# Pooled attention into a Mish FFN: the row maximum in two chains, its transposes in row tiles, and part of the row sums on TensorE

## Chip, cores and metric

The kernel runs on one core of one Trainium2 chip. The metric is device time in microseconds (us) of one execution, without host work.

## What is computed

```python
def _attn_ref(q, k, v):                     # q, k, v: (4, 8, 1152, 64) float32
    q_pool = q.reshape(B, H, S // 2, 2, D).mean(axis=3)
    scores = (1.0 / np.sqrt(D)) * np.matmul(q_pool, k.transpose(0, 1, 3, 2))
    scores = scores - np.max(scores, axis=-1, keepdims=True)
    attn = np.exp(scores)
    attn = attn / (np.sum(attn, axis=-1, keepdims=True) + 1e-09)
    return np.matmul(attn, v)

def _moe_ref(x, w_in, w_out):               # x: (2304, 512), d_ff = 2048
    h = x @ w_in
    sp = np.where(h > 20.0, h, np.log1p(np.exp(np.minimum(h, 20.0))))
    return (h * np.tanh(sp)) @ w_out
```

Neighbouring queries are averaged in pairs, so each of the 32 (batch, head) pairs has 576 queries and 1152 keys. The attention output, its heads side by side, is the input of the FFN.

## The kernel before

**Attention.** There are 32 steps. A step `i` takes two heads (`j` = 0, 1, on the partition halves 0 to 63 and 64 to 127 of the inputs) and half of their queries (288 columns, `HQ`). Scores are made transposed: keys on partitions, queries along the free axis. The 1152 keys are nine chunks `c` of 128. For each chunk TensorE computes `s` (`QK`, 128 x 2 x 288, two PSUM banks), with the two heads in the two 64-row halves of the array; ScalarE copies it into `T3` in SBUF (`CP`); VectorE folds it into a running maximum `rmax` (`MX`). Two PSUM tiles (`psS`) hold scores, so a chunk's scores need the copy and the maximum of an earlier chunk done.

The maximum over keys runs across partitions. So `MT` transposes the 576 columns of `rmax` on TensorE in five blocks of 128, `TMAX` reduces them on VectorE to a column `m`, and `MB`/`MBb` transpose `m`, broadcast along the free axis, back into a PSUM tile `Mb` that holds each query's maximum on all 128 partitions. `SUB` subtracts it (VectorE, in four groups of 2, 2, 2 and 3 chunks), `EXP` exponentiates on ScalarE, `PV` multiplies by the values on TensorE (two column halves, again one for each head). GpSimd (POOL) adds the nine chunks of exponentials together (`ADD` 0 to 4, the last two of half width), `FIN0` sums that over the partitions with a matmul by ones, and `FLN`, `FEX`, `FE`, `FU`, `FX` divide and write into `xT`.

**FFN.** After step 31 come 18 blocks of 256 tokens by 16 slices of d_ff, in float32r with hi and lo parts: `H_` (12 matmuls), `A_g`/`A_gh` (Mish on ScalarE), `D_gl`, `O_` (6 matmuls). Some of the weight conversion (`conv`) and of the splitting of `xT` (`split_h`, `split_l`) lies between attention steps.

**What sets the order.** The order on every engine is written out by hand: `STEP` gives for each function of a step its time, in units of one step, for even and odd `i`; `FILL` overrides it for the first steps, `END` for the last. All entries are sorted by time and issued in that order; each engine then works its own queue from front to back and waits only for semaphores. An instruction that waits on TensorE therefore holds up all matmuls behind it. A warm-up (`first`) keeps TensorE busy until the first inputs are there.

The fold that the change rewrites is a single chain:

```python
def MX(i, c):
    if c == 1:
        rmaxs[i, 1] = p2.tile([P, 2, HQ], F32, tag="rmax", name=f"rmax{i}")
    r = rmaxs[i, 1]
    dve.tensor_tensor(r, ss[i, c], T3[:, i % 2, 0] if c == 1 else r, ALU.max)
```

Of the kernel before, what the change touches and what calls it, by code (L numbers as in the profile page):

```python
# [22 lines left out]
def tile_pooled_attention_then_mish_ffn(ctx: ExitStack, tc: tile.TileContext, q, k, v, moe_w_in, moe_w_out, out):  # L23
# [42 lines left out]
    if True:  # L66
# [60 lines left out]
        WARM2 = ((64, 64), (64, 64), (64, P), (64, 64), (P, 64), (64, 64))  # L127

        def first():
            qk_tiles(0)  # L130
            if NWARM:
# [3 lines left out]
                x = ps1.tile([P, 2, 512], F32, tag="Mb", name="warm2")  # L135
                for k, m in WARM2:
                    for r in range(0, P, k):
                        for c in range(0, P, m):
                            pe.matmul(x[c:c + m, r // 64, 0:P], ident[r:r + k, 0:m], ident[r:r + k], start=True, stop=True)
# [776 lines left out]
```

## Time and profile before

| | |
|---|---|
| three runs | 854.29, 854.6 and 857.56 us, median 854.6 |
| the profiled execution | 854.77 us, of which the span from first to last instruction is 852.7 us |
| attention, until the last step's maximum | 0 to 428 us |
| change-over and FFN | 428 to 852.7 us |
| busy over the span | PE 97%, PEld 67%, DVE 70%, ACT 60%, POOL 53% |
| the same from 150 to 200 us | PE 98%, DVE 98%, POOL 96%, ACT 88% |

PE is the matmuls of TensorE and PEld its weight loads, DVE is VectorE, ACT is ScalarE, POOL is GpSimd. In the attention stage nearly every engine is busy nearly all the time, in the FFN stage only PE is. Matmuls are pipelined, so the distance from the start of one group to the start of the next says more than a busy share: a group of matmuls that waits counts as busy.

### The profile page before, as it was taken

Reading aid. Unit: us, or ns where it says so; the run is one execution under the profiler, and the core shown is the slowest. Engines: PE = TensorE matmul, PEld = TensorE weight load, DVE = VectorE, ACT = ScalarE, POOL = GpSimd, SP = SyncE. Lnnn points to the kernel's source line nnn. Section 1 sums busy time; section 2 is a strip of 40 time slices with the busy share of each in tenths; the row PEclk is TensorE's granted clock in tenths of the full one; section 3 lists DMA queues with packets and bytes.
Section 4 is the critical chain, followed back from the end, with each engine's and each line's share of the span. In section 5 each row is a group of like instructions: output and inputs, shape, how many; then the busy total and the mean of one; then the engine's idle time right before and its main releaser. Section 6 shows DMA issues by size and latency. Waiting matters only on the chain. (4 is left out here: it accounts for less than half of the span.)

```text
span 852.7 us, 13965 instructions
## 1 busy us (share of the span) xinstructions
PE 826.5 (97%) x5422; PEld 572.9 (67%) x5422; DVE 592.7 (70%) x810; ACT 513.0 (60%) x916; POOL 449.8 (53%) x268
## 2 busy tenths in 40 slices
PE   7899999999999999999989999999999999999997
PEld 4344444444444444444468899999999999989896
DVE  6999999999999999999978634444553444422222
ACT  5788898888888888988865643333333333222221
POOL 0799999999999999999876401110111101100000
PEclk9899999999999999999999999999999999999999
DMA  5320122211222202222001111110211111001102
GB/s 213 109 83 15 71 84 84 84 41 44 85 84 85 74 13 83 84 84 78 1 1 50 59 41 50 50 50 25 75 50 50 50 48 34 20 26 50 45 30 74
DMA packets 16913, 50.70 MB, mean 59 GB/s; under 512 B 1616, under 2 KB 6480, under 8 KB 16848
## 3 DMA queue, kind: packets, MB, share of 16 engines
q1 hardware_dynamic: 16848, 49.81, 16.9%
q8 instruction: 43, 0.70, 0.3%
q14 instruction: 22, 0.18, 0.1%
HBM read 45.09 MB, written 4.72 MB: 58 GB/s over the span
## 5 line engine op out<-in xcount | busy, mean ns | idle before, releaser
L742 DVE TENSOR_TENSOR gl<-g,gh 128x256 fp32r<-128x256 f32 x144 | 67.3, 467 | 226.1 <-ACT gh L737 199.9
L154 PE MATMUL s<-qT,kT 64*128 64x288 f32 x1152 | 200.1, 449 | 7.3 <-DVE rmax L171 3.2
L164 ACT COPY T<-s 128x576 f32<-128x576 f32 x288 | 180.2, 635 | 40.5 <-DVE rmax L171 24.0
L732 ACT ACTIVATE g<-h 128x256 f32<-128x256 f32 x144 | 55.7, 387 | 244.7 <-PE h L727 244.7
L204 DVE TENSOR_TENSOR T<-T,Mb 128x1152 f32<-128x1152 f32 (+1 forms) x128 | 191.2, 1495 | 0.9 <-PE Mb L198 0.9
L208 ACT ACTIVATE T<-T 128x1152 f32<-128x1152 f32 (+1 forms) x128 | 164.4, 1286 | 25.4 <-DVE T L204 25.2
L226 PE MATMUL pv<-T,vn 128*64 128x288 f32 x1152 | 174.5, 420 | 3.5 <-ACT pvs L237 3.5
L171 DVE TENSOR_TENSOR rmax<-s,rmax 128x576 f32<-128x576 f32 x224 | 168.6, 753 | 11.1 <-ACT T L164 1.8
L405 POOL TENSOR_TENSOR wl<-wt,wh 128x512 fp32r<-128x512 f32 x32 | 41.9, 1308 | 247.1 <-ACT wh L402 203.2
L216 POOL TENSOR_TENSOR acc<-acc,T 128x1152 f32<-128x1152 f32 x64 | 169.0, 2640 | 6.0 <-ACT T L208 3.1
L727 PE MATMUL h<-xh,wh 128*128 128x256 f32 x576 | 162.1, 281 | 0.0
L727 PE MATMUL h<-xh,wl 128*128 128x256 f32 x576 | 161.8, 281 | 0.0
L727 PE MATMUL h<-xl,wh 128*128 128x256 f32 x576 | 161.6, 281 | 0.0
L154 PEld LDWEIGHTS s<-qT,kT 64*128 64x128 f32 x1152 | 91.8, 189 | 99.7 <-ACT T L164 49.4
L226 PEld LDWEIGHTS pv<-T,vn 128*64 128x64 f32 x1152 | 71.7, 137 | 80.4 <-issue 42.2
L727 PEld LDWEIGHTS h<-xh,wh 128*128 128x128 f32 x576 | 108.7, 189 | 8.0 <-issue 1.3
L727 PEld LDWEIGHTS h<-xl,wh 128*128 128x128 f32 x576 | 108.8, 189 | 6.0
L727 PEld LDWEIGHTS h<-xh,wl 128*128 128x128 f32 x576 | 109.2, 189 | 0.0
L214 POOL TENSOR_TENSOR acc<-T 128x1152 f32<-128x1152 f32 x32 | 84.7, 2648 | 21.1 <-ACT gh L737 6.0
L760 PE MATMUL o<-wh,gh 128*128 128x512 f32 x146 | 57.8, 396 | 1.0 <-ACT xT L772 1.0
L760 PE MATMUL o<-wl,gh 128*128 128x512 f32 x146 | 57.6, 394 | 0.0
L760 PE MATMUL o<-wh,gl 128*128 128x512 f32 x146 | 57.3, 392 | 0.0
(373 smaller groups left out, 987.1 us busy)
## 6 DMA issues: line engine op xcount, KB each, us to landing
vn<-in_v_dram SPq DMA_DIRECT2D x16, 576.0 KB, 6.3
kT<-in_k_dram SPq DMA_DIRECT2D x15, 576.0 KB, 5.0
qn<-in_q_dram SPq DMA_DIRECT2D x15, 576.0 KB, 3.8
ri<-in_moe_w_in_dram SPq DMA_DIRECT2D x16, 512.0 KB, 3.5
ro<-in_moe_w_out_dram SPq DMA_DIRECT2D x16, 512.0 KB, 3.5
out_dram<-xT SPq DMA_DIRECT2D x18, 256.0 KB, 2.6
qh<-in_q_dram SPq DMA_DIRECT2D x2, 288.0 KB, 5.0
kT<-in_k_dram SPq DMA_DIRECT2D x1, 256.0 KB, 4.7
```

The source lines that it names most:

```text
L154: pe.matmul(s[:, j, 0:HQ], kT[64 * j:64 * j + 64, c], qT[64 * j:64 * j + 64, hf], start=True, stop=True,)
L164: act.copy(T3[:, i % 2, c], ss[i, c])
L171: dve.tensor_tensor(r, ss[i, c], T3[:, i % 2, 0] if c == 1 else r, ALU.max)
L204: dve.tensor_tensor(x, x, Mbs[i][:, :, 0:HQ].unsqueeze(1).to_broadcast([P, w, 2, HQ]), ALU.subtract)
L208: act.activation(x, x, AF.Exp, scale=0.0625)
L214: pool.tensor_tensor(accs[i], t[:, 0:2], t[:, 2:4], ALU.add)
L216: pool.tensor_tensor(accs[i], accs[i], t[:, 2 * n + 2:2 * n + 4], ALU.add)
L226: pe.matmul(pvs[i][64 * j:64 * j + 64, 0:HQ], vn[:, j, c, :], T3[:, i % 2, c, j], start=(pvn[i] == 1), stop=(pvn[i] == NC),)
L727: pe.matmul(h[:, 0:UT], a, b, start=(m == 0), stop=(m == len(seq) - 1))
L732: act.activation(g, hs[bu, f], AF.Mish)
L742: dve.tensor_tensor(gl, ch.pop((bu, f)), f32(gs[bu, f][0]), ALU.subtract)
L760: pe.matmul(os_[bu][t], x, y, start=(first and m == 0), stop=(last and m == 2))
```

## The change

1. **Two chains.** Chunks 1, 3, 5, 8 are folded into `rmax0` (seeded with the copied chunk 0), chunks 4 and 6 into `rmax1` (seeded with the copied chunk 2). `MX` of chunk 7 takes `rmax1` and writes its result over the scores of chunk 7 in PSUM; `MXF` folds that into `rmax0`. A step still has eight maxima.
2. **Transposes in row tiles.** `MT` becomes ten transposes of 64 partitions x 128 columns, two for each block, in the two 64-row halves of the array. It takes every fourth column of `rmax` for blocks 0 to 3. `MB` (with `MBb` merged into it) becomes nine such transposes that write every fourth column of `Mb`; `Mb` is now 576 columns in a row. `TMAX` and `SUB` read the new layouts.
3. **Sums.** POOL makes only `ADD` 0, 1, 2. The two halves of the accumulator and chunk 8 of `T3` are summed over partitions by three matmul pairs (`FIN0`, `FIP1`, `FIP0`) that accumulate in one PSUM tile, where there was one pair.
4. **Order.** `STEP` is written anew, with the same times for even and odd steps nearly everywhere and the score chunks mostly in pairs; `FILL`, the pooling of `q` (`QP`), the loads of `q`, the splits (`XE`, `XL`) and the release of PSUM (`REUSE`) have new times. The warm-up is 19 transposes where it was 6 transposes and 20 small matmul instructions.

```diff
-    NWARM = 6
+    NWARM = 19
...
-        WARM2 = ((64, 64), (64, 64), (64, P), (64, 64), (P, 64), (64, 64))
...
+        CHAIN, SEED, FOLD = ((1, 3, 5, 8), (4, 6, 7)), (0, 2), 7
+        PIECES = 2
...
         def MX(i, c):
-            if c == 1:
-                rmaxs[i, 1] = p2.tile([P, 2, HQ], F32, tag="rmax", name=f"rmax{i}")
-            r = rmaxs[i, 1]
-            dve.tensor_tensor(r, ss[i, c], T3[:, i % 2, 0] if c == 1 else r, ALU.max)
-
-        MBLK = (0, 128, 224, 352, 448)
+            n = [c in a for a in CHAIN].index(True)
+            first = c == CHAIN[n][0]
+            if first:
+                rmaxs[i, n] = p2.tile([P, 2, HQ], F32, tag=f"rmax{n}", name=f"rmax{i}_{n}")
+            r = rmaxs[i, n]
+            x = r
+            if first:
+                x = T3[:, i % 2, SEED[n]]
+            dve.tensor_tensor(ss[i, c] if c == FOLD else r, ss[i, c], x, ALU.max)
+
+        def MXF(i):
+            r = rmaxs[i, 0]
+            dve.tensor_tensor(r, ss[i, FOLD], r, ALU.max)
...
         def MT(i):
-            rm = rmaxs.pop((i, 1)).rearrange("p a b -> p (a b)")
-            t = ps1.tile([P, 1024], F32, tag="Mb", name=f"mt{i}")
-            for n, a in enumerate(MBLK):
-                pe.transpose(t[:, n * P:(n + 1) * P], rm[:, a:a + P], ident)
+            rm = rmaxs.pop((i, 0)).rearrange("p a b -> p (a b)")
+            t = ps1.tile([P, 2, 512], F32, tag="Mb", name=f"mt{i}")
+            for n in range(5):
+                for r in range(2):
+                    h = slice(64 * r, 64 * r + 64)
+                    x = rm[h, n:4 * P:4] if n < 4 else rm[h, W - P:W]
+                    pe.transpose(t[:, r, 64 * n:64 * n + 64], x, ident[h, h])
...
         def MB(i):
             m = Ts.pop(i)
-            Mb = ps1.tile([P, 2, 512], F32, tag="Mb", name=f"Mb{i}")
-            Mbs[i] = Mb, m
-            for n, j, a in ((0, 0, 0), (1, 0, 128), (3, 1, 64), (4, 1, 160)):
-                pe.transpose(Mb[:, j, a:a + P], m[:, n:n + 1].to_broadcast([P, P]), ident)
-
-        def MBb(i):
-            Mb, m = Mbs[i]
-            for k, j, a in ((0, 0, 224), (64, 1, 0)):
-                pe.transpose(Mb[:, j, a:a + 64], m[k:k + 64, 2:3].to_broadcast([64, P]), ident[k:k + 64, k:k + 64])
-            Mbs[i] = Mb
+            Mb = ps1.tile([P, 1024], F32, tag="Mb", name=f"Mb{i}")
+            for n in range(5):
+                for r in range(n // 4, 2):
+                    h = slice(64 * r, 64 * r + 64)
+                    a = 256 + 256 * r + n
+                    x = Mb[:, a:256 + a - n:4] if n < 4 else Mb[:, 768:832]
+                    pe.transpose(x, m[h, n:n + 1].to_broadcast([64, P]), ident[h, h])
+            Mbs[i] = Mb[:, 256:832]
...
-                pool.tensor_tensor(accs[i][:, 0], accs[i][:, 0], t[:, 8] if n == 3 else accs[i][:, 1], ALU.add)
+                pool.tensor_tensor(accs[i][:, 0], accs[i][:, 0], t[:, 8] if n + PIECES == 3 else accs[i][:, 1], ALU.add)
...
+        def SUM(i, a, n):
...
+            for j in range(2):
+                pe.matmul(fin[i][64 * j:64 * j + 64, 0:HQ], ones, a[:, j], start=(n == 0), stop=(n == PIECES))
+
+        def FIP0(i):
+            SUM(i, T3[:, i % 2, 8], 0)
+
+        def FIP1(i):
+            SUM(i, accs[i][:, 1], 1)
+
         def FIN0(i):
...
+            SUM(i, accs.pop(i)[:, 0], PIECES)
...
-            (MX, 7, 0.2982, 0.2113),
+            (MX, 7, 0.3034, 0.3034),
...
-        LW, REUSE = -0.5, -0.544
+        LW, REUSE = -0.5, -0.678
```

What that makes of the order shows best on the two engines that are fullest. The rows below are one step in the middle of the attention stage. On VectorE (`L204` and `L208` are `SUB`, `L263` and `L275` `FE`, `L282` `FX`, `L185` and `L191` `TMAX`), before, from the maximum's reduction on:

```order
L185 TENSOR_REDUCE m_1648<-mt_1637 128x5
L171 TENSOR_TENSOR rmax_1643<-s_2_1645,rmax_1643 128x576
L282 SCALAR_TENSOR_TENSOR xT<-Sb_1602,pvs_1590 128x288
L204 TENSOR_TENSOR T_98<-T_98,Mb_1654 128x1152
L171 TENSOR_TENSOR rmax_1643<-s_3_1664,rmax_1643 128x576
L204 TENSOR_TENSOR T_98<-T_98,Mb_1654 128x1152
L171 TENSOR_TENSOR rmax_1643<-s_4_1678,rmax_1643 128x576
L171 TENSOR_TENSOR rmax_1643<-s_5_1682,rmax_1643 128x576
L204 TENSOR_TENSOR T_98<-T_98,Mb_1654 128x1152
L171 TENSOR_TENSOR rmax_1643<-s_6_1698,rmax_1643 128x576
L171 TENSOR_TENSOR rmax_1643<-s_7_1705,rmax_1643 128x576
L171 TENSOR_TENSOR rmax_1643<-s_8_1724,rmax_1643 128x576
```

and on the same engine after:

```order
L191 TENSOR_REDUCE m_1799<-mt_1783 128x5
L170 TENSOR_TENSOR rmax_0_1781<-s_3_1796,rmax_0_1781 128x576
L170 TENSOR_TENSOR rmax_1_1818<-s_4_1802,T_98 128x576
L208 TENSOR_TENSOR T_98<-T_98,Mb_1806 128x1152
L170 TENSOR_TENSOR rmax_0_1781<-s_5_1830,rmax_0_1781 128x576
L170 TENSOR_TENSOR rmax_1_1818<-s_6_1833,rmax_1_1818 128x576
L208 TENSOR_TENSOR T_98<-T_98,Mb_1806 128x1152 x2
L170 TENSOR_TENSOR rmax_0_1781<-s_8_1859,rmax_0_1781 128x576
L170 TENSOR_TENSOR s_7_1854<-s_7_1854,rmax_1_1818 128x2x288
L174 TENSOR_TENSOR rmax_0_1781<-s_7_1854,rmax_0_1781 128x576
```

Of two maxima in a row the second used to read what the first had just written; now that is so only in the last pair of a step, chunk 7 and `MXF`. On TensorE (`L154` and `L149` are the scores, `L226` and `L230` `PV`, `L180` and `L185` `MT`, `L193`, `L198` and `L202` `MB`, `L248` and `L252` the sums; `x2` are the two matmuls of one chunk), before:

```order
L180 MATMUL mt_1637<-identr,rmax_1538 128x128 x5
L154 MATMUL s_2_1645<-qT_1450,kT_1451 128x288 x2
L193 MATMUL Mb_1654<-identr,m_1648 128x128 x4
L198 MATMUL Mb_1654<-identr,m_1648 128x64 x2
L154 MATMUL s_3_1664<-qT_1450,kT_1451 128x288 x2
L226 MATMUL pv_1598<-T_98,vn_1495 64x288 x4
L154 MATMUL s_4_1678<-qT_1450,kT_1451 128x288 x2
L154 MATMUL s_5_1682<-qT_1450,kT_1451 128x288 x2
L226 MATMUL pv_1598<-T_98,vn_1495 64x288 x6
```

and after:

```order
L149 MATMUL s_2_1900<-qT_1578,kT_1579 128x288 x2
L185 MATMUL mt_1907<-identr,rmax_0_1781 128x64 x10
L149 MATMUL s_3_1920<-qT_1578,kT_1579 128x288 x2
L149 MATMUL s_4_1926<-qT_1578,kT_1579 128x288 x2
L202 MATMUL Mb_1930<-identr,m_1923 128x64 x9
L230 MATMUL pv_1868<-T_98,vn_1620 64x288 x4
L149 MATMUL s_5_1950<-qT_1578,kT_1579 128x288 x2
L149 MATMUL s_6_1954<-qT_1578,kT_1579 128x288 x2
L230 MATMUL pv_1868<-T_98,vn_1620 64x288 x4
L252 MATMUL Sb_1965<-T_98,cst 64x288 x2
L252 MATMUL Sb_1965<-acc_1871,cst 64x288 x2
```

Scores, `MT` and `MB` now stand together in one stretch of 64-row instructions, where before each of them stood between others of another shape; two more pairs of sums stand beside the `PV`. At the start of the program, TensorE ran before (`L134` and `L139` are the warm-up):

```order
L134 MATMUL warm<-identr 128x128 x6
L139 MATMUL warm_114<-identr 64x128 x8
L139 MATMUL warm_114<-identr 128x128 x2
L139 MATMUL warm_114<-identr 64x128 x10
L154 MATMUL s_0_143<-qT_105,kT_106 128x288 x2
```

and it runs now:

```order
L132 MATMUL warm<-identr 128x128 x19
L149 MATMUL s_0_135<-qT_105,kT_106 128x288 x2
L149 MATMUL s_1_138<-qT_105,kT_106 128x288 x2
L149 MATMUL s_2_144<-qT_105,kT_106 128x288 x2
L149 MATMUL s_3_151<-qT_105,kT_106 128x288 x2
```

The warm-up is 19 transposes in a row, and the first scores follow them directly.

## Rows read from the trace of the kernel before

**Rows 1.** Busy time by stretch, all engines: us, busy us (instructions), clock, DMA.
```profile
20.00:40.00 20.00, 17.23 (x93) 7.76 (x95) 18.20 (x23) 14.42 (x20) 14.90 (x9) 0.83 0.35 115
...
150.00:200.00 50.00, 48.98 (x336) 24.17 (x332) 48.95 (x58) 43.92 (x64) 48.05 (x28) 1.00 0.21 72
...
420.00:440.00 20.00, 15.36 (x117) 9.62 (x114) 16.34 (x16) 14.18 (x22) 15.10 (x10) 1.00 0.00 1
...
550.00:600.00 50.00, 50.00 (x323) 45.25 (x321) 22.33 (x43) 16.63 (x45) 6.37 (x5) 1.00 0.16 53
```
**Rows 2.** The line of `TMAX`, steps 3 to 31: count, durations, first and last start.
```profile
L185 DVE TENSOR_REDUCE m<-mt x29: 812/815/826, 61.6 to 428.1; 128x5 f32<-128x640 f32 x29
```
**Rows 3.** VectorE in order of time within one step: start, length, line, instruction, count.
```profile
216.03 1.94 DVE L204 TENSOR_TENSOR T<-T,Mb 128x1728 f32<-128x1728 f32 x1
217.89 0.46 DVE L263 SCALAR_TENSOR_TENSOR Sb<-Sb,rs 128x288 f32<-128x288 f32 x1
218.26 0.74 DVE L171 TENSOR_TENSOR rmax<-s,T 128x576 f32<-128x576 f32 x1
218.92 0.81 DVE L185 TENSOR_REDUCE m<-mt 128x5 f32<-128x640 f32 x1
219.65 0.74 DVE L171 TENSOR_TENSOR rmax<-s,rmax 128x576 f32<-128x576 f32 x1
220.32 0.45 DVE L282 SCALAR_TENSOR_TENSOR xT<-Sb,pvs 128x288 f32<-128x288 f32 x1
220.69 1.35 DVE L204 TENSOR_TENSOR T<-T,Mb 128x1152 f32<-128x1152 f32 x1
221.96 0.75 DVE L171 TENSOR_TENSOR rmax<-s,rmax 128x576 f32<-128x576 f32 x1
...
223.88 1.61 DVE L171 TENSOR_TENSOR rmax<-s,rmax 128x576 f32<-128x576 f32 x2
225.41 1.34 DVE L204 TENSOR_TENSOR T<-T,Mb 128x1152 f32<-128x1152 f32 x1
```
**Rows 4.** TensorE in order of time, three places of the attention stage.
```profile
204.45 0.71 PE L226 MATMUL pv<-T,vn 128*64 128x288 f32 x4
205.09 0.77 PE L180 MATMUL mt<-identr,rmax 128*128 128x128 f32 x5
205.78 1.24 PE L154 MATMUL s<-qT,kT 64*128 64x288 f32 x8
206.96 0.65 PE L193 MATMUL Mb<-identr,m 128*128 128x128 f32 x4
207.54 0.27 PE L198 MATMUL Mb<-identr,m 64*128 64x64 f32 x2
207.74 0.71 PE L226 MATMUL pv<-T,vn 128*64 128x288 f32 x4
...
209.67 2.16 PE L226 MATMUL pv<-T,vn 128*64 128x288 f32 x16
211.76 1.24 PE L154 MATMUL s<-qT,kT 64*128 64x288 f32 x8
...
220.37 0.27 PE L198 MATMUL Mb<-identr,m 64*128 64x64 f32 x2
220.48 0.70 PE L154 MATMUL s<-qT,kT 64*128 64x288 f32 x4
```
**Rows 5.** One of GpSimd's half-width adds, grouped by line, 60 to 400 us.
```profile
L218 POOL TENSOR_TENSOR acc<-acc 128x576 f32<-128x576 f32 x26 | 36.8, 1417 | 2.0
```
**Rows 6.** The start, in order of time: warm-up, first scores, a stall of VectorE.
```profile
1.62 1.00 PE L134 MATMUL warm<-identr 128*128 128x128 f32 x6 [1.62 <-DVE cst L72]
...
6.24 3.61 PE L154 MATMUL s<-qT,kT 64*128 64x288 f32 x16
...
31.21 0.76 DVE L171 TENSOR_TENSOR rmax<-s,rmax 128x576 f32<-128x576 f32 x1 [1.80 <-ACT T L164]
```
**Rows 7.** TensorE where attention gives way to the FFN.
```profile
437.38 2.16 PE L226 MATMUL pv<-T,vn 128*64 128x288 f32 x16 [3.03 <-ACT pvs L237]
```

More of the change, by code (lines that the diff above doesn't have):

```diff
@@ L134, in first @@
                     pe.transpose(x[:, n % 4], identr, identr)
[L135 to L139, printed above, removed]
         rmaxs, Mbs, pvs, pvn, accs = {}, {}, {}, {}, {}
+        CHAIN, SEED, FOLD = ((1, 3, 5, 8), (4, 6, 7)), (0, 2), 7
+        PIECES = 2
         def chunks(i, g):
@@ L239, in tile_pooled_attention_then_mish_ffn @@
         fin = {}
-        def FIN0(i):
-            a = accs.pop(i)[:, 0]
-            if i < NS - 1:
-                Sb = ps1.tile([P, 512], F32, tag="x", name=f"Sb{i}")
-            else:
-                Sb = pools["psH"].tile([P, 512], F32, tag="h", name=f"Sb{i}")
-            for j in range(2):
-                pe.matmul(Sb[64 * j:64 * j + 64, 0:HQ], ones, a[:, j], start=True, stop=True)
-            fin[i] = Sb
+        def SUM(i, a, n):
+            if n == 0:
+                if i < NS - 1:
+                    fin[i] = ps1.tile([P, 512], F32, tag="x", name=f"Sb{i}")
+                else:
+                    fin[i] = pools["psH"].tile([P, 512], F32, tag="h", name=f"Sb{i}")
+            for j in range(2):
[4 more added lines that the diff above has]
+            SUM(i, accs[i][:, 1], 1)
+        def FIN0(i):
+            SUM(i, accs.pop(i)[:, 0], PIECES)
         def FLN(i):
@@ new lines, in tile_pooled_attention_then_mish_ffn @@
+            (MT, 0.6257, 0.6257),
+            (TMAX, 0.6822, 0.6822),
+            (MB, 0.7511, 0.7511),
+            (SUB, 0, 0.8454, 1.0507),
+            (EXP, 0, 0.9556, 1.1609),
+            (SUB, 1, 1.0507, 0.8454),
+            (SUB, 2, 1.1507, 1.1507),
+            (EXP, 1, 1.1609, 0.9556),
+            (PV, 2, 1.2632, 1.2632),
+            (ADD, 0, 1.2839, 1.2839),
+            (PV, 3, 1.3016, 1.3784),
+            (PV, 0, 1.3400, 1.3400),
+            (EXP, 2, 1.3582, 1.3860),
+            (PV, 1, 1.3784, 1.3016),
@@ new lines, in tile_pooled_attention_then_mish_ffn @@
+            (0.450, load_w, 3),
+            (0.457, CP, 0, 8),
+            (0.461, MX, 1, 3),
+            (0.473, MT, 0),
+            (0.476, conv, 1, 5),
+            (0.512, QK, 1, 4),
+            (0.520, TMAX, 0),
+            (0.559, QK, 1, 5),
+            (0.577, MX, 1, 4),
+            (0.579, QP, 1),
+            (0.597, MB, 0),
+            (0.630, MX, 1, 5),
+            (0.641, CP, 1, 4),
+            (0.683, SUB, 0, 1),
+            (0.694, CP, 1, 5),
+            (0.694, conv, 0, 5),
@@ new lines, in tile_pooled_attention_then_mish_ffn @@
+            (1.103, EXP, 0, 3),
+            (1.117, PV, 0, 1),
+            (1.136, MX, 1, 7),
+            (1.156, PV, 0, 3),
+            (1.188, load_v, 1),
+            (1.188, conv, 2, 1),
+            (1.194, PV, 0, 0),
+            (1.225, CP, 1, 8),
+            (1.236, MXF, 1),
+            (1.238, PV, 0, 8),
+            (1.288, SUB, 0, 2),
+            (1.300, QK, 2, 0),
+            (1.347, QK, 2, 1),
+            (1.366, CP, 2, 0),
+            (1.388, conv, 2, 2),
+            (1.393, PV, 0, 6),
@@ L684, in tile_pooled_attention_then_mish_ffn @@
+            (4.563, ADD, 3, 1),
+            (9.616, FX, 7),
         ]
```

564 lines of the change are left out of this document (223 added, 341 removed).

## The prediction

> **What bounds the kernel now.** I read the busy time by stretch first. The FFN is bound by TensorE alone, which is busy for 50.00 of 50 us there, and the change doesn't touch it. In the middle of attention four engines are nearly full at once: TensorE 48.98, VectorE 48.95, GpSimd 48.05 and ScalarE 43.92 of 50 us [rows 1]. So the next view is the length of a step, from the line that runs once in each: `TMAX` starts at 61.6 in step 3 and at 428.1 in step 31, so 28 steps take 366.5 us, **13.09 us a step** [rows 2]. Attention is half of the time and the change acts on each step, so a tenth of a microsecond a step is worth 2.8 us.
>
> Which engine sets the 13.09 I read from start to start, in order of time. On VectorE a `SUB` of two chunks holds the engine 1.27 us (220.69 to 221.96), one of three chunks 1.86, a maximum 0.66 to 0.67, `TMAX` 0.73, `FE` and `FX` 0.37 each. The reader is to see one exception: two maxima in a row, the second reading what the first wrote, take 1.53 until the next instruction (223.88 to 225.41), so the first holds the engine 1.53 - 0.67 = 0.86. A maximum after another instruction's result costs 0.67, one after its own chain's costs 0.19 more [rows 3]. Two steps hold five such pairs. VectorE's sum for a step is 8 x 0.67 + 0.73 + 2 x 0.37 + 3 x 1.27 + 1.86 = 12.50, and 5/2 x 0.19 = 0.48 on top: 12.98 of 13.09. **VectorE sets the step**, with 0.11 us of true waiting.
>
> For TensorE I take runs of one shape. A run of one `PV` chunk takes 0.64 (204.45 to 205.09), one of four 2.09 (209.67 to 211.76): 0.483 a chunk and 0.16 for the run itself. Two chunks of scores take 1.18, 0.20 more than 2 x 0.483. `MT` takes 0.69 and the four large transposes of `MB` 0.58; the two small ones of `MBb`, in the two row halves and with scores behind them, take 0.11 together (220.37 to 220.48) [rows 4]. Two steps have 38 chunks (18 scores, 18 `PV`, 2 sums), 12 runs of scores, 9 of `PV` and sums, 2 `MT`, 2 `MB`, 2 `MBb`: 18.35 + 2.40 + 1.44 + 1.38 + 1.16 + 0.22 = 24.95, or 12.5 a step. It has 0.6 us to spare, although its busy share is the same as VectorE's. GpSimd's share of 0.96 is 12.6 us a step.
>
> **The two chains.** The number of maxima stays at eight, the widths stay, and four of the five dependent pairs in two steps part; one pair a step is left (chunk 7, `MXF`). VectorE's sum becomes 12.50 + 0.19 = 12.69. What the trace doesn't show is a maximum that writes to PSUM. Nearest is `FE`, which does, beside `FX`, which writes SBUF: 0.37 both [rows 3]. I take nothing for it, with 0.1 as upper end. `TMAX` still reads 640 elements and `SUB` as many as before: nothing.
>
> **Transposes and runs on TensorE.** A step now has four runs of scores (one of them with all 19 transposes in it) and four of `PV` and sums: 16 runs in two steps where there were 25. It has 21 chunks, since two pairs of sums are added. The price of a strided transpose in a 64-row half isn't in the trace. Its bounds: 0.05 us a pair, if a pair costs half of one of 128 columns ((0.69 - 0.16) / 5 = 0.11); 0.22, if the two don't overlap and each costs 0.11. I take 0.11, from the one row that has a pair of this shape with scores behind it [rows 4]. Then a step is 21 x 0.483 + 4 x 0.20 + 4 x 0.16 + 9.5 x 0.11 = 10.14 + 0.80 + 0.64 + 1.05 = **12.6** (12.1 to 13.7 between the bounds). So TensorE isn't relieved: nine runs fewer in two steps give back 0.8 a step, the added sums take 0.97. It is now as full as VectorE.
>
> **Sums off GpSimd.** Two adds of 1.42 a step go [rows 5]: 12.6 becomes 9.8. Nothing waits for GpSimd for long, so by itself this gains nothing; it takes the third full engine out of the way, which the tighter order needs. ScalarE keeps its instructions, 11.5 us a step.
>
> **The new order's waits.** TensorE's queue now holds scores behind `MB`, and `MB` waits for `TMAX`. From the start of `TMAX` to chunk 5's maximum VectorE itself needs 0.73 + 2 x 0.67 + 1.27 = 3.34 us. The way over TensorE is 0.82 for the reduction [rows 2], 0.5 for `MB`, 1.12 for the run of two chunks behind it and 0.70 for the scores of chunk 5 [rows 4], with some 0.2 of hand-overs: 3.3 to 3.4. No slack there, none to spare on TensorE's own sum, so the step won't quite reach VectorE's 12.69. Before, it lay 0.11 above; I take 0.06, a step of **12.75 us**. The gain is 28 x (13.09 - 12.75) = 9.5 us.
>
> **Start.** The first scores come at 6.24, right behind the warm-up, whose six transposes take 1.00 us from 1.62 on [rows 6]. Nineteen end near 4.8 at that rate, so scores can start up to 2 us earlier; but the chain goes on to weights and the second half of `q`, which come no earlier. On the other side stands the stretch from 20 to 40 us, where the granted clock averages 0.83 and VectorE stalls 1.80 us for a copy [rows 1, 6]: a new order there can lose or win that. I take a gain of 1.0 us, between a gain of 3 and a loss of 2.
>
> **End.** Steps 30 and 31 add two sums each, 2 x 0.97 = 1.9 us, to a TensorE that is full from 437 us on. Ahead of that it waits 3.03 us [rows 7]; there the two splits on VectorE now come before the first `SUB`, into a wait, and I count 1 us of TensorE's wait back, and a little for GpSimd's shorter adds. Net a loss of 0.5, between a gain of 1 and a loss of 1.9.
>
> **Sum.** The profiled execution took 854.77 us (span 852.7, 2.1 around it), within 0.02% of the median of the three runs. 854.8 - 9.5 - 1.0 + 0.5 = **844.8 us**.
>
> **Rivals.** (a) *The transposes don't overlap.* Reads and writes with a step of four elements run at half rate, a pair costs 0.22, TensorE needs 13.7 and sets the step with some 0.1 of waits: 13.8 x 28 is 20 us more than now, 874 us. From 0.14 us a pair on, the gain is gone; if only `MB` suffers the step is near 13.25, and the time 859. For it speaks that no matmul of before reads or writes with a step; against it, that the unstepped pair in the two halves costs 0.11, no more than one full transpose. The Trainium skill has a rule for this case: "PSUM — Partial Sum Buffer", section "Specifications (TRN2)", says that any non-contiguous access pattern slows matmuls significantly. No run here shows it yet; by that rule at least `MB`'s eight stepped writes pay. Its chance is 0.13. (b) *TensorE takes VectorE's place.* At 12.6 of 12.75 every stop of its queue counts: scores that wait for their buffer begin a new run (0.1 us more). Three or four of these a step give 13.0 to 13.05: the gain is 1 to 3 us, near 852 us. Before, TensorE stopped often, but with 0.6 us to spare. Chance 0.15. (c) *The floor is reached.* The pairs cost 0.05, TensorE has 0.5 us to spare, the step is 12.69 or a little less: 28 x 0.41 = 11.5, 842 us. Chance 0.2. (d) *The chains don't part the maxima.* The 0.19 belongs to something else than the dependence: 12.98 stays, and the time is near 852. Against it: a maximum that starts a new chain right behind another instruction costs 0.66. Chance 0.04.
>
> **How the numbers follow.** The forecast, a step of 12.7 to 12.9, gives 842 to 850 us and has 0.48. About 0.5% of the time, 4.3 us, is what a measurement tells from no change, so faster means below 850.3: the forecast, (c) and a little of (b) and (d), 0.74. Within 0.5%: most of (b) and (d), the milder (a), 0.15. Slower: the rest of (a), 0.11. The range takes in (c) with a good start, 840, and (b) with a bad start and end, 857; it leaves out most of (a) and little else.
>
> **What would show it.** In the profile after, `TMAX` should come every 12.7 to 12.8 us; the maxima on VectorE should follow each other at 0.67 apart except for one pair a step; ten transposes of `MT` should take 0.55 us and nine of `MB` 0.5; GpSimd's share should fall to about 0.77 and TensorE stay full. The prediction fails if the transposes take 1 us or more each time, if VectorE shows idle time behind scores or `MB`, or if step 3 comes later than 62 us.

## The result, and the profile after

| | before | after | predicted |
|---|---|---|---|
| median of four runs | 854.64 us (854.29 to 857.56) | 843.54 us (842.96 to 846.37) | 844.8 us (840 to 857) |
| ratio, with its 95% interval | | 0.9869 (0.9838 to 0.9901) | 0.988 |
| profiled execution: start to `TMAX` of step 3 | 61.6 us | 62.3 us (+0.7) | -1.0 |
| from there to `TMAX` of step 31 | 366.5 us | 355.2 us (-11.3) | -9.5 |
| from there to the end | 424.6 us | 427.1 us (+2.5) | +0.5 |

The change makes the kernel 1.3% faster. The profiled execution of after took 846.37 us (span 844.6) and is the longest of its four; the other three have spans of 841.2 to 842.2 us. Only the longest has a trace.

The line of `TMAX` in the kernel after, as in [rows 2] (count, durations, first and last start):

```profile
L191 DVE TENSOR_REDUCE m<-mt x29: 814/816/826, 62.3 to 417.5; 128x5 f32<-128x640 f32 x29
```

28 steps take 355.2 us, 12.69 us each, where they took 13.09. The middle steps take 12.70 each; the last one, 12.11, pulls the mean down. The stretches to hold against [rows 1] (us, then busy us and instructions of PE, PEld, DVE, ACT and POOL, the granted clock of TensorE as a share of 2.4 GHz, DMA share, GB/s); the last is a part of the one above it:

```profile
0.00:20.00 20.00, 14.45 (x87) 9.06 (x89) 12.30 (x21) 11.42 (x18) 3.18 (x9) 0.89 0.68 244
20.00:40.00 20.00, 16.99 (x108) 8.46 (x106) 17.28 (x21) 13.39 (x19) 9.88 (x5) 0.77 0.29 97
150.00:200.00 50.00, 50.00 (x410) 28.10 (x408) 49.72 (x60) 44.67 (x66) 37.96 (x20) 1.00 0.21 72
420.00:440.00 20.00, 17.08 (x108) 11.50 (x105) 12.55 (x13) 11.06 (x19) 7.93 (x4) 0.83 0.00 1
...
428.00:432.00 4.00, 4.00 (x18) 2.56 (x15) 0.85 (x2) 3.14 (x6) 0.00 (x0) 0.50 0.00 0
```

In the middle GpSimd fell from 48.05 to 37.96 of 50 us and TensorE rose to 50.00. At both ends the granted clock is lower than before: 0.89 for 1.00 and 0.77 for 0.83 in the first two stretches, 0.83 for 1.00 in the last. The first stretch before:

```profile
0.00:20.00 20.00, 15.99 (x111) 9.21 (x111) 11.63 (x21) 10.85 (x17) 1.50 (x7) 1.00 0.63 227
```

One step on VectorE after, to hold against [rows 3] (start, length, engine, line, instruction, count):

```profile
146.36 0.76 DVE L170 TENSOR_TENSOR s<-s,rmax 128x576 f32<-128x576 f32 x1
147.15 0.76 DVE L174 TENSOR_TENSOR rmax<-s,rmax 128x576 f32<-128x576 f32 x1
147.83 1.94 DVE L208 TENSOR_TENSOR T<-T,Mb 128x1728 f32<-128x1728 f32 x1
149.69 0.46 DVE L275 SCALAR_TENSOR_TENSOR Sb<-Sb,rs 128x288 f32<-128x288 f32 x1
150.18 0.76 DVE L170 TENSOR_TENSOR rmax<-s,T 128x576 f32<-128x576 f32 x1
...
154.54 1.41 DVE L170 TENSOR_TENSOR rmax<-s,rmax 128x576 f32<-128x576 f32 x2
155.88 2.60 DVE L208 TENSOR_TENSOR T<-T,Mb 128x1152 f32<-128x1152 f32 x2
```

Two maxima of different chains take 1.34 until the next instruction (154.54 to 155.88), twice 0.67, where a pair of one chain took 1.53 [rows 3]. The last pair, chunk 7 through PSUM and `MXF`, takes 1.47 (146.36 to 147.83). One gap is left: `FE` at 149.69 holds the engine 0.37, and chunk 1's maximum starts 0.49 after it. So VectorE has 12.58 us of work in a step of 12.70 and waits 0.12 in one place, for chunk 1.

What that maximum waits for shows when one step is followed across the engines. The rows are of one step after, one fence for each engine:

```profile
158.09 0.71 PE L252 MATMUL Sb<-acc,cst 128*64 128x288 f32 x4
...
163.06 0.64 PE L185 MATMUL mt<-identr,rmax 64*128 64x64 f32 x10
163.69 1.24 PE L149 MATMUL s<-qT,kT 64*128 64x288 f32 x8
164.79 0.50 PE L202 MATMUL Mb<-identr,m 64*128 64x64 f32 x9
165.22 0.71 PE L230 MATMUL pv<-T,vn 128*64 128x288 f32 x4
...
170.81 0.70 PE L252 MATMUL Sb<-acc,cst 128*64 128x288 f32 x4
```

```profile
158.98 2.65 POOL L218 TENSOR_TENSOR acc<-T 128x1152 f32<-128x1152 f32 x1 [3.42 <-ACT T L159]
```

```profile
161.67 1.18 ACT L159 COPY T<-s 128x576 f32<-128x576 f32 x2 [0.40 <-POOL acc L218]
```

```profile
162.88 0.76 DVE L170 TENSOR_TENSOR rmax<-s,T 128x576 f32<-128x576 f32 x1
```

`FIN0` (158.09, ended 158.80) reads the only accumulator; then `ADD` 0 may write it (158.98). Its row names a copy, but that one ended 0.04 us before, nearer than any hand-over; from `FIN0`'s end it is 0.18, the same 0.18 as in the run further down whose row names the sums (175.89 to 176.07). `ADD` 0 is the last reader of chunks 0 and 1 in that half of `T3`, so their copies start at 161.67. Chunk 1's maximum starts when they end, at 162.88, and sets free the scores' buffer for the run that starts at 163.69. Behind that run `MB`, `PV`, scores and sums stand back to back until `FIN0` comes again at 170.81. The legs are 0.89 + 2.69 + 1.21 + 0.81 + 7.12 = 12.72: **a ring over four engines is as long as the step.** 7.1 us of it is TensorE's queue. That is a reading; the runs below test it.

### The profile page after: what moved, and what is told of

It is laid out like the page before. It is cut to its first block, busy times and chain, and to the rows that moved or that the text cites. A ratio compares the mean times of both kernels' runs of the same rounds, so it can differ in the third digit from the quotient of the medians.

```text
span 844.6 us, 14807 instructions
## 1 busy us (share of the span) xinstructions
PE 825.5 (98%) x5907; PEld 600.9 (71%) x5907; DVE 586.1 (69%) x810; ACT 508.8 (60%) x916; POOL 359.5 (43%) x204
## 4 chain that ended last, share of the span: by engine, by line
PE 93%; DVE 3%; ACT 2%; DMA 1%; issue 1%; SPq 0%; DVEq 0%; ACTq 0%
PE h L664 24%; PE s L149 19%; PE pv L230 17%; PE o L697 12%; PE Sb L252 6%; PE mt L185 2%; DVE T L208 1%; PE Mb L202 1%; ACT T L212 1%; DMA ri<-in_moe_w_in_dram 1%; DVE rmax L170 1%; ACT T L159 1%; PE o43pv L697 0%; PE o41pv L697 0%; PE o37pv L697 0%
## 5 line engine op out<-in xcount | busy, mean ns | idle before, releaser
L679 DVE TENSOR_TENSOR gl<-g,gh 128x256 fp32r<-128x256 f32 x144 | 63.5, 441 | 229.7 <-ACT gh L674 203.6
L159 ACT COPY T<-s 128x576 f32<-128x576 f32 x288 | 176.6, 636 | 38.9 <-PE s L149 21.7
L149 PE MATMUL s<-qT,kT 64*128 64x288 f32 x1152 | 188.2, 441 | 5.3 <-DVE rmax L170 2.0
L208 DVE TENSOR_TENSOR T<-T,Mb 128x1152 f32<-128x1152 f32 (+1 forms) x128 | 188.5, 1494 | 0.0
L230 PE MATMUL pv<-T,vn 128*64 128x288 f32 x1152 | 170.5, 423 | 4.1 <-ACT pvs L241 2.9
L149 PEld LDWEIGHTS s<-qT,kT 64*128 64x128 f32 x1152 | 96.6, 189 | 83.6 <-ACT T L159 52.2
L230 PEld LDWEIGHTS pv<-T,vn 128*64 128x64 f32 x1152 | 75.6, 139 | 71.3 <-issue 21.9
L170 DVE TENSOR_TENSOR rmax<-s,rmax 128x576 f32<-128x576 f32 x128 | 93.3, 748 | 0.4 <-PE s L149 0.2
```

The source lines that it names most:

```text
L149: pe.matmul(s[:, j, 0:HQ], kT[64 * j:64 * j + 64, c], qT[64 * j:64 * j + 64, hf], start=True, stop=True,)
L159: act.copy(T3[:, i % 2, c], ss[i, c])
L170: dve.tensor_tensor(ss[i, c] if c == FOLD else r, ss[i, c], x, ALU.max)
L208: dve.tensor_tensor(x, x, Mbs[i].unsqueeze(1).to_broadcast([P, w, W]), ALU.subtract)
L230: pe.matmul(pvs[i][64 * j:64 * j + 64, 0:HQ], vn[:, j, c, :], T3[:, i % 2, c, j], start=(pvn[i] == 1), stop=(pvn[i] == NC),)
L679: dve.tensor_tensor(gl, ch.pop((bu, f)), f32(gs[bu, f][0]), ALU.subtract)
```

## The experiments

All runs but one (the chains alone) change the kernel after; steps are read from the line of `TMAX` in each run's trace. `fills` was executed four times and `best` five times, the others once. Four executions of the kernel after lie 3.4 us apart, so of a single run the step says more than the total.

**Undoing the chains.** The same instructions in the same order, with other chunks in the chains:

```diff
-        CHAIN, SEED, FOLD = ((1, 3, 5, 8), (4, 6, 7)), (0, 2), 7
+        CHAIN, SEED, FOLD = ((1, 3, 4, 5, 6, 8), (7,)), (0, 2), 7
```

> The changed kernel with the chunks spread otherwise over the chains: chunks 1, 3, 4, 5, 6 and 8 in the first, chunk 7 alone in the second. The instructions, their order and their sizes stay the same; only chunk 4 now reads what chunk 3 has just written, and chunk 6 what chunk 5 has. Theory (VectorE sets the step, and a maximum that depends on the one before costs 0.19 us more): two more dependent pairs a step, step 12.70 + 0.38 = 13.08 us, last TMAX 10.6 us later, about 854 us. Rival (the 0.19 us belongs to something else, the gain came from the order or from TensorE): the step stays 12.70 and the time 841 to 846 us.

Measured: 850.77 us, a step of 12.95. VectorE, the same place as above:

```profile
139.77 1.61 DVE L170 TENSOR_TENSOR rmax<-s,rmax 128x576 f32<-128x576 f32 x2
141.30 1.34 DVE L208 TENSOR_TENSOR T<-T,Mb 128x1152 f32<-128x1152 f32 x1
...
150.61 0.46 DVE L275 SCALAR_TENSOR_TENSOR Sb<-Sb,rs 128x288 f32<-128x288 f32 x1
150.98 0.75 DVE L170 TENSOR_TENSOR rmax<-s,T 128x576 f32<-128x576 f32 x1
```

Both pairs are back at 1.53 (139.77 to 141.30, and 142.56 to 144.09 likewise), so the 0.19 us is the dependence: rival (d) of the prediction falls. The step isn't 12.70 + 0.38 but 12.58 + 0.38 = 12.96: the 0.12 us in front of chunk 1 is gone (150.61 to 150.98 is 0.37), and VectorE sets the step. In the kernel after, then, something else does.

**Transposes in unit steps.** `MT` takes neighbouring columns, `MB` writes neighbouring columns:

```diff
-                    x = rm[h, n:4 * P:4] if n < 4 else rm[h, W - P:W]
+                    x = rm[h, n * P:n * P + P] if n < 4 else rm[h, W - P:W]
...
-                    a = 256 + 256 * r + n
-                    x = Mb[:, a:256 + a - n:4] if n < 4 else Mb[:, 768:832]
+                    a = 256 + 256 * r + 64 * n
+                    x = Mb[:, a:a + 64] if n < 4 else Mb[:, 768:832]
```

> The changed kernel with unit steps in place of every fourth column: MT takes 128 neighbouring columns of the maxima and MB writes 64 neighbouring columns of Mb (still two PSUM banks for the two row halves). The maxima thereby land on other queries, so that part of the computation is changed. Theory (a step of four elements costs nothing here): ten transposes of MT in 0.49 to 0.62 us and nine of MB in 0.43 to 0.44 us from start to the next instruction, as with steps; step 12.70 us, 841 to 846 us. Rival (stepped patterns slow a transpose): MB falls to 0.3 us or less; the step can fall only to what VectorE needs, 12.69.

Measured: 844.58 us, step 12.69 as before this edit. Weight loads of `MT` grouped by line, 62 to 410 us, count, busy us and mean ns; first the kernel after, then this one:

```profile
L185 PEld LDWEIGHTS mt<-identr,rmax 64*128 64x128 f32 x270 | 19.0, 195 | 2.5
```

```profile
L185 PEld LDWEIGHTS mt<-identr,rmax 64*128 64x128 f32 x270 | 12.8, 138 | 4.0
```

`MB`'s stepped writes to PSUM cost nothing: from the first of the nine transposes to what follows it is 0.43 us in the kernel after (164.79 to 165.22) and 0.43 here (151.35 to 151.78, below). `MT`'s stepped reads do cost: the maxima are what TensorE loads as weights, and a load takes 195 ns instead of 138. Both theories had the wrong one of the two in mind. And though `MT` is shorter, the step isn't; the run of scores behind it now waits:

```profile
149.62 0.47 PE L185 MATMUL mt<-identr,rmax 64*128 64x64 f32 x10
150.25 1.24 PE L149 MATMUL s<-qT,kT 64*128 64x288 f32 x8 [0.15 <-DVE rmax L170]
151.35 0.50 PE L202 MATMUL Mb<-identr,m 64*128 64x64 f32 x9
151.78 0.95 PE L230 MATMUL pv<-T,vn 128*64 128x288 f32 x6
```

It waits for chunk 1's maximum (start 149.44 in this run), 0.81 us behind it as in the kernel after. So TensorE isn't simply full: what it does between that maximum and the scores behind it lies beside the ring.

**The old kind of transposes**, at the same places of the order; `MB` and the reading in `TMAX` change likewise:

```diff
-            t = ps1.tile([P, 2, 512], F32, tag="Mb", name=f"mt{i}")
+            t = ps1.tile([P, 1024], F32, tag="Mb", name=f"mt{i}")
             for n in range(5):
-                for r in range(2):
-                    h = slice(64 * r, 64 * r + 64)
-                    x = rm[h, n:4 * P:4] if n < 4 else rm[h, W - P:W]
-                    pe.transpose(t[:, r, 64 * n:64 * n + 64], x, ident[h, h])
+                x = rm[:, n * P:n * P + P] if n < 4 else rm[:, W - P:W]
+                pe.transpose(t[:, n * P:n * P + P], x, ident)
...
```

> The changed kernel with the old kind of transposes: MT is five of 128 x 128 and MB four of 128 x 128 and one of 64 x 128, in unit steps, at the same places of the order, and so between scores of the two-row-half shape. TensorE's sum for a step after the change is 21 x 0.483 + 8 runs (1.44) + 0.49 + 0.44 = 12.5 us. Theory (the row shape is needed to keep TensorE below VectorE's 12.69): 0.69 + 0.69 in place of 0.93 and three more starts of a run at 0.2 each, about 13.5, so a step of 13.1 to 13.5 us and 855 to 866 us. Rival (TensorE has room, the shape is worth nothing): step up to 12.8 us, 841 to 848 us.

Measured: 859.09 us, a step of 13.24.

```profile
154.19 0.77 PE L183 MATMUL mt<-identr,rmax 128*128 128x128 f32 x5
154.88 1.24 PE L149 MATMUL s<-qT,kT 64*128 64x288 f32 x8
156.06 0.85 PE L198 MATMUL Mb<-identr,m 128*128 128x128 f32 x5
156.83 1.19 PE L226 MATMUL pv<-T,vn 128*64 128x288 f32 x8
```

From the scores behind `MT` to the end of `MB` it is 1.95 us (154.88 to 156.83), where it was 1.53 (163.69 to 165.22); and those scores come 0.97 behind the start of chunk 1's maximum (153.91), not 0.81, since `MT` now ends after that maximum. 0.42 + 0.16 = 0.58 us, about the 0.55 by which the step grew. So the row shape is worth about 0.55 us a step, somewhat more than half of what the two added pairs of sums cost by the prediction (0.97). At 12.51 us, by the sum that stood in the expectation, TensorE would have had 0.2 us to hide it in; it had none.

**The sums back on GpSimd**, all of them:

```diff
-        PIECES = 2
+        PIECES = 0
...
-            (FIP0, 1.8236, 2.0434),
...
-            (FIP1, 2.0818, 2.0818),
...
-            (FIN0, 2.2207, 2.2207),
...
+            (ADD, 3, 2.0400, 2.0400),
+            (ADD, 4, 2.1500, 2.1500),
+            (FIN0, 2.3030, 2.3030),
...
```

> The changed kernel with the whole row sum back on GpSimd: five adds a step as before the change, one pair of sums on TensorE, FIN0 and FLN 1 us later in the order. GpSimd's sum is 9.8 + 2 x 1.42 = 12.6 us a step, TensorE's 12.5 - 0.97 = 11.5. Theory (the sums had to move because a third engine as full as the step holds the others up): step 12.8 to 12.95 us, 845 to 851 us. Rival (VectorE alone sets the step, GpSimd just fits): step 12.70 us, with GpSimd's share at 0.99, 841 to 846 us. Below 12.69 neither expects it.

Measured: 896.72 us, steps of 14.03 and 14.98 in turn (14.41 on the mean), which neither expected. `FIN0` runs from 175.23 to 175.89; then, engine by engine:

```profile
176.07 2.65 POOL L218 TENSOR_TENSOR acc<-T 128x1152 f32<-128x1152 f32 x1 [1.92 <-PE Sb L252]
```

```profile
178.75 1.18 ACT L159 COPY T<-s 128x576 f32<-128x576 f32 x2 [1.20 <-POOL acc L218]
```

```profile
179.96 0.76 DVE L170 TENSOR_TENSOR rmax<-s,T 128x576 f32<-128x576 f32 x1 [1.37 <-ACT T L159]
```

Here the profile names the ring itself: `ADD` 0 waits for `FIN0`, the copies for `ADD` 0, chunk 1's maximum for the copies. GpSimd is busy 43.86 of 50 us and waits for its own sum to be read. Two adds of 1.42 us stand ahead of `FIN0`, and I had put `FIN0` later besides, so this run doesn't price GpSimd's work; it shows the ring at work when `FIN0` comes late.

**The chains alone**, in the kernel before: chunks 1, 3, 5, 7 and 4, 6, 8, with `MXF` a maximum of two SBUF tiles.

```diff
...
-            r = rmaxs[i, 1]
-            dve.tensor_tensor(r, ss[i, c], T3[:, i % 2, 0] if c == 1 else r, ALU.max)
...
+            r = rmaxs[i, n]
+            dve.tensor_tensor(r, ss[i, c], T3[:, i % 2, 2 * n] if first else r, ALU.max)
+
+        def MXF(i):
+            r = rmaxs[i, 0]
+            dve.tensor_tensor(r, r, rmaxs.pop((i, 1)), ALU.max)
...
```

> The kernel before with the two chains alone: chunks 1, 3, 5, 7 in one and 4, 6, 8 in the other (seeded with the copied chunks 0 and 2), and a last maximum MXF of the two in SBUF; the old transposes, sums, warm-up and order, with chunk 2's maximum gone and MXF put behind chunk 8's. Eight maxima a step as before. VectorE's sum falls from 12.98 to 12.6 or 12.7. Theory (TensorE at 12.5, GpSimd at 12.6 and the old order's hand-overs stand close behind, so the chains alone give only a part): step 12.8 to 13.0 us, 846 to 852 us. Rival (VectorE alone set the step): step 12.70 us as in the changed kernel, 843 to 846 us. Second rival (the chains give nothing in the old order): 13.09 us, 855 us.

Measured: 903.48 us, a step of 14.70 on the mean (14.2 to 15.8). None of the three. Two groups of VectorE, 75 to 450 us (count, busy us, mean ns, idle us ahead and what ended it):

```profile
L173 DVE TENSOR_TENSOR rmax<-s,rmax 128x576 f32<-128x576 f32 x128 | 94.4, 753 | 12.1 <-PE s L154 6.1 <-ACT T L164 2.4
L177 DVE TENSOR_TENSOR rmax<-rmax,rmax 128x576 f32<-128x576 f32 x26 | 36.1, 1388 | 0.9
```

`MXF` takes 1388 ns, nearly twice a maximum with a PSUM operand (753). That is 0.6 of the 1.6 us; the rest are waits of the old order, which I didn't take apart. What the chains alone would bring in the old order stays open.

**The fold in SBUF, later**, in the kernel after:

```diff
-            dve.tensor_tensor(ss[i, c] if c == FOLD else r, ss[i, c], x, ALU.max)
+            dve.tensor_tensor(r, ss[i, c], x, ALU.max)
...
-            dve.tensor_tensor(r, ss[i, FOLD], r, ALU.max)
+            dve.tensor_tensor(r, r, rmaxs.pop((i, 1)), ALU.max)
...
-            (MXF, 0.3717, 0.3717),
+            (MXF, 0.5500, 0.5500),
```

> The changed kernel with chunk 7 folded into the second chain in SBUF and MXF (the maximum of the two chains, now SBUF with SBUF) moved behind SUB 3, so that it no longer reads what the instruction before it wrote. In the changed kernel VectorE's own instructions sum to 12.58 us of the 12.70 us step, and chunk 1's maximum waits 0.12 us for scores; the whole_rows run grew by just what its transposes and runs add on TensorE (0.54 us). Theory (TensorE now sets the step, by the sum 12.6 to 12.7): VectorE gets 0.13 us free and waits that much longer, step 12.68 to 12.72 us, 841 to 846 us. Rival (VectorE still sets it): step 12.55 to 12.6 us, 3 to 4 us less, 837.5 to 842 us. Third, if a maximum of two SBUF operands is dearer or MT comes too late behind it: 12.8 us or more.

Measured: 852.72 us, steps of 12.71 and of 13.11, the third case of the expectation. Two of its `MXF`, and GpSimd beside them:

```profile
154.96 0.75 DVE L174 TENSOR_TENSOR rmax<-rmax,rmax 128x576 f32<-128x576 f32 x1
...
167.67 1.41 DVE L174 TENSOR_TENSOR rmax<-rmax,rmax 128x576 f32<-128x576 f32 x1
```

```profile
155.04 1.31 POOL L290 TENSOR_TENSOR pvs<-pvs,rs 128x288 f32<-128x288 f32 x1
...
167.67 0.80 POOL L290 TENSOR_TENSOR pvs<-pvs,rs 128x288 f32<-128x288 f32 x1
168.43 3.16 POOL L220 TENSOR_TENSOR acc<-acc,T 128x1152 f32<-128x1152 f32 x1
```

The two engines take turns. Where `MXF` came first (154.96) it took 0.75, and GpSimd's multiplication of 0.80 took 1.31. Where that came first (167.67), `MXF` took 1.41, and the add behind took 3.16 instead of 2.65. The Trainium skill states it in "GPSIMD Engine Reference", section "1. Specifications": GpSimd's SBUF interfaces are shared with VectorE and contend with VectorE instructions that have two SBUF inputs. These rows agree. Early on it is worse: the `MXF` at 62.15 found an add of 2.62 us begun 0.13 before, took 3.10, and the steps there are 15.32 and 14.02 long. The fold through PSUM avoids that: in the kernel after, every maximum between 60 and 400 us has one operand in PSUM, and each takes 0.74 to 0.76 us, with GpSimd's adds beside it or not. In the steps with a short `MXF` VectorE had 0.13 us less to do, and they still took 12.71: VectorE didn't set the step.

**One pair of sums off TensorE**, first in the kernel after, then together with the late fold:

```diff
-        PIECES = 2
+        PIECES = 1
...
+            (ADD, 3, 1.8280, 1.8280),
...
-            (FIP1, 2.0818, 2.0818),
...
```

> The changed kernel with one of the two added pairs of sums taken off TensorE again: the two halves of the accumulator are added on GpSimd (1.42 us, right behind ADD 2), FIP1 is gone. GpSimd goes from 9.8 to 11.2 us a step, TensorE loses 0.5 to 0.58. Theory (TensorE sets the step): the step falls to what VectorE needs, 12.58 to 12.62 us, 2 to 3.4 us less, 838 to 843 us. Rival (VectorE sets it): 12.70 us, 841 to 846 us. Third (GpSimd's later FIN0 holds the next ADD 0 and the copies behind it): 12.8 us or more.

> Both edits together: MXF in SBUF behind SUB 3, and FIP1 back on GpSimd. TensorE's sum is 12.1 us, VectorE's 12.45, GpSimd's 11.2, ScalarE's 11.5. Theory (the step is the fuller of TensorE and VectorE plus 0.05 to 0.1 of waits): 12.47 to 12.55 us, 4.2 to 6.4 us less than the changed kernel, 835 to 841 us, while each edit alone gives less than half of that. Rival (the way from TMAX over MB and two runs of scores to chunk 5's maximum, 3.3 to 3.4 us, or another loop sets the step): 12.6 to 12.7 us, 839 to 845 us.

Measured: 842.19 us with steps of 12.57 and 12.79 in turn. Both together took 847.37 us, outside the theory: steps are 12.53, as it had it, where `MXF` came first (0.74 us), but 12.86 where it came behind GpSimd's multiplication (1.16), and step 3 comes 2.1 us later than in the kernel after, behind one `MXF` of 2.67. With one pair less, 0.58 us of TensorE's queue (169.06 to 169.64 in the kernel after) leave the ring, and every second step falls by 0.13 to VectorE's own 12.57, as the theory had it. In the other steps GpSimd also pools `q` and splits `x`. GpSimd and VectorE of the one-piece kernel:

```profile
168.60 0.73 POOL L644 TENSOR_TENSOR xl<-xT,xh 128x256 fp32r<-128x256 f32 x1
169.30 1.42 POOL L122 TENSOR_TENSOR qT<-qn 128x576 f32<-128x576 f32 x1
170.68 2.64 POOL L218 TENSOR_TENSOR acc<-T 128x1152 f32<-128x1152 f32 x1
```

```profile
173.98 0.46 DVE L275 SCALAR_TENSOR_TENSOR Sb<-Sb,rs 128x288 f32<-128x288 f32 x1
174.56 0.76 DVE L170 TENSOR_TENSOR rmax<-s,T 128x576 f32<-128x576 f32 x1
```

`ADD` 0 comes without a gap behind the pooling, so it is late by GpSimd's own queue, and chunk 1 waits 0.21 us (0.58 behind `FE` instead of 0.37). That leg can be eased too, by moving the split:

```diff
-        XL = 1.143
+        XL = 2.143
```

> The one_piece kernel with the splits' second half (XL, one 0.73 us instruction of GpSimd in some steps) a step later, so that it no longer falls in the steps in which GpSimd also pools q. In one_piece those steps take 12.79 us, the others 12.57: GpSimd comes to ADD 0 later there, the copies behind it wait, and chunk 1's maximum waits 0.2 us. Theory (GpSimd's row is what is late in every second step): the long steps fall to 12.57 to 12.65, 0.8 to 1.5 us less in all, 840.5 to 842 us. Rival (pooling q alone, 1.41 us, still makes ADD 0 late, or VectorE is held elsewhere): steps stay 12.75 or more, 842 us.

Measured: 837.59 us; after step 3 every step but the last takes 12.57, and `FE` and chunk 1's maximum stand 0.37 apart in all of them. The gain is larger than both sides expected, 4.6 us against the one-piece kernel: 0.09 us in each of 28 steps are 2.6 of it; the rest lies in the start (`TMAX` of step 3 at 61.0, 0.6 earlier) and after the last `TMAX`, where the granted clock from 420 to 440 us was 1.00 in this run and 0.91 in that one.

**The start.** The changed kernel with the old warm-up:

```diff
-    NWARM = 19
+    NWARM = 6
+    WARM2 = ((64, 64), (64, 64), (64, P), (64, 64), (P, 64), (64, 64))
...
```

> The changed kernel with the old warm-up: six transposes and 20 small matmuls, so that the first scores come near 6.2 us instead of 4.2. All else as changed. Theory (the earlier scores gained nothing, since weights, the second half of q and the clock set the start): TMAX of step 3 within 0.5 us of 62.3, steps 12.70, 841 to 846 us. Rival (the warm-up gained the 1 to 2 us that the first scores come earlier, and the new order lost it again): TMAX of step 3 at 63.3 us or later, 843 to 848 us.

Measured: 845.18 us. `TMAX` of step 0 comes at 20.6 instead of 19.1, that of step 3 at the same 62.3 us. So the longer warm-up gains nothing that lasts to step 3. The two don't run at one clock, though: from 0 to 20 us the granted clock is 1.00 here and 0.89 in the kernel after, from 20 to 40 us 0.74 and 0.77. What the earlier scores would be worth at an even clock isn't shown.

**The clock.** Where TensorE waits, in the first 27 us and ahead of the last step's `PV`, transposes that nobody reads:

```diff
+        def still(n, tag):
+            x = ps1.tile([P, 4, P], F32R, tag=tag, name=f"still{len(stills)}")
+            stills.append(x)
+            for k in range(n):
+                pe.transpose(x[:, k % 4], identr, identr)
...
+        plan += [(NS + 0.245, still, 24, "x")]
+        plan += [(t, still, n, "pv") for t, n in ((-0.28, 5), (-0.139, 10), (0.472, 14), (0.946, 16), (1.0745, 8))]
```

> The changed kernel with transposes that nobody reads put into TensorE's waits: 24 before the first PV of the last step (TensorE waits 2.92 us there), and 5, 10, 14, 16 and 8 into five waits of the first 27 us. Nothing else changes. In the changed kernel the granted clock falls to half after these waits: 0.77 on the mean from 20 to 40 us, 0.83 from 420 to 440, where the 16 matmuls behind the wait take 4.11 us instead of 2.1. Theory (the clock falls because TensorE waited, and that costs time at both ends): no stretch of 420 to 440 us below 1.00, from the last TMAX to the end 423.5 to 424.5 us instead of 427.1; in the start the clock above 0.9 on the mean and TMAX of step 3 at 58 to 61 us instead of 62.3; median 838 to 841.5 us. Rival (the start is bound by loads, copies and VectorE, and most executions have no dip at the end): TMAX of step 3 within 0.5 us of 62.3, median 842 to 844 us. Third (the fillers delay the matmuls behind them): later than 62.8, median above 844.

Measured: median 840.69 us (840.07 to 841.49), ratio to before 0.9832 (0.9811 to 0.9853). The stretches of this kernel, then the 16 matmuls behind the last wait, in the kernel after and in this one:

```profile
20.00:40.00 20.00, 17.68 (x144) 9.69 (x142) 20.00 (x25) 15.50 (x22) 11.68 (x6) 1.00 0.31 105
...
420.00:440.00 20.00, 19.09 (x146) 15.19 (x145) 15.29 (x13) 12.78 (x24) 10.65 (x6) 1.00 0.00 1
```

```profile
426.11 4.11 PE L230 MATMUL pv<-T,vn 128*64 128x288 f32 x16 [2.92 <-ACT pvs L241]
```

```profile
420.24 2.17 PE L138 MATMUL still<-identr 128*128 128x128 f32 x24
423.31 2.16 PE L237 MATMUL pv<-T,vn 128*64 128x288 f32 x16 [0.91 <-ACT pvs L248]
```

With TensorE kept busy the granted clock stays at 1.00, its level of 2.4 GHz. `TMAX` of step 3 comes at 59.5 us, 2.8 earlier, and from the last `TMAX` to the end it is 424.3 us instead of 427.1. In the kernel after TensorE waited 2.92 us there and then worked at 0.50, 1.2 GHz. Before, it waited 3.03 us at the same place [rows 7] and kept 1.00, so in these two traces one such wait cost the clock and one didn't.

**All that helped, together**: one pair less, the splits a step later, the fillers.

> The one_piece_xl kernel with the fillers of the fills run: one pair of sums less on TensorE, the splits' second half a step later, and transposes that nobody reads in TensorE's waits of the first 27 us and before the last step's PV. The changed kernel's median is 843.54 us, one_piece_xl took 837.59, fills 840.69. Theory (the two gains lie in different stretches and add up): steps of 12.57 us, TMAX of step 3 at 59 to 60 us (60.96 in one_piece_xl), 423.3 to 424 us from the last TMAX to the end, clock 1.00 throughout; median 835.5 to 837 us. Rival (the start's gain is lost in the first steps' hand-overs, since one_piece_xl's start was already 1.3 us earlier than the changed kernel's): TMAX of step 3 near 61, median 837.3 to 838.5 us.

Measured: median **836.25 us** (835.81 to 836.46), ratio to before 0.9783 (0.977 to 0.9797). The time is the theory's, 0.9% under the changed kernel's median; the clock is 1.00 from 0 to 40 and from 420 to 440 us.

```profile
L198 DVE TENSOR_REDUCE m<-mt x29: 817/817/826, 59.1 to 410.6; 128x5 f32<-128x640 f32 x29
```

## Why the prediction was right, and where it wasn't

The time, 843.54 us, is 1.3 us under the forecast. Term by term it is less good, and two things came that the prediction had named as signs of failing: step 3 came later than 62 us, at 62.3, and VectorE idles once a step, though behind copies and not behind scores or `MB`.

- **What bounds before.** The 0.19 us of a dependent maximum, read from one pair of rows [rows 3], is confirmed by undoing it (one_chain). VectorE's sum explained the 13.09 to within a tenth.
- **The chains.** With the new order but two more dependent pairs the step is 12.95; so 0.14 of the 0.40 us a step comes from the order and what goes with it, and 0.26 from parting the pairs. That split is rough: one_chain has three dependent pairs a step where before had two and a half, and the 0.38 that two pairs cost shows only in part, because the ring holds the kernel after. VectorE's own work is 12.58, not the 12.69 of the sum, partly because the last pair, through PSUM, costs 0.13 and not 0.19.
- **The transposes.** 0.11 us a pair gave 1.05 us a step; `MT` and `MB` together take 0.63 + 0.43 = 1.06. The sum was right, the even price wasn't: `MB`'s four and a half pairs cost 0.096 each, `MT`'s five 0.126, because of their weight loads. Rival (a) fell: 0.22 a pair is seen nowhere. The rule cited for it, in "PSUM — Partial Sum Buffer", section "Specifications (TRN2)" of the Trainium skill, doesn't hold for `MB`'s writes, 0.43 us for the nine with and without steps (plain_blocks). What a step slows here is a load from SBUF, 195 instead of 138 ns.
- **The step.** I forecast 12.75, VectorE's 12.69 and 0.06 of waits around `TMAX`, `MB` and chunk 5. It came to 12.70 in the middle, but as 12.58 and 0.12 of waits in front of chunk 1. Of the 1.8 us that the steps gained beyond the forecast, 0.6 is the last step alone (12.11). The way from `TMAX` to chunk 5 that I held for the tight one isn't late anywhere. I missed the ring `FIN0`, `ADD` 0, copies, chunk 1's maximum, scores. I had written that GpSimd's relief gains nothing by itself because nothing waits for GpSimd for long; where its `ADD` 0 starts is one leg of that ring. So rival (b) was the nearer mechanism, TensorE's queue in VectorE's place, at a price of a tenth of a microsecond instead of the 0.3 that I gave it. A step below (c)'s floor of 12.69 was had by another way, 12.57 in one_piece_xl; (c)'s own sum, 854.8 - 11.5 - 1.0 + 0.5, gives 842.8 us and not 842.
- **The start.** A gain of 1.0 was forecast, a loss of 0.7 measured: the step that failed. The earlier first scores left nothing by step 3 (old_warm), and the clock, which I named as the other side and then priced at nothing, is worth 2.8 us (fills). The kernel before lost time to its own dip there (0.83 from 20 to 40 us), and no run takes that out; how much of the 0.7 is the clock's stays open.
- **The end.** A loss of 0.5 was forecast. With the clock held it is 424.3 us against 424.6 before, a gain of 0.3, so the added sums cost nothing that shows. In the profiled execution the clock's dip costs 2.8 us there. The other three are 2.4 to 3.4 us shorter, with a mean granted clock of 0.992 to 0.994 over the span where the profiled one has 0.986; where in the span theirs was low isn't shown. In old_warm, which has the same end, the clock was 0.91 from 420 to 440 us and the end took 425.9.

Without that dip the steps came out 1.8 us better than forecast, the start 1.7 worse and the end 0.8 better; so near a hit is partly luck. So is the step: 12.70 stands close to the forecast 12.75, but the ring sets it and not VectorE.
